# A replanned attention stage: other groups, other engines for two operations, zeros written in parts

## The chip, the cores and the metric

The kernel runs on one core of one Trainium2 chip. The metric is device time in microseconds (us) of one execution. TensorE (PE; PEld is its weight load) multiplies matrices, VectorE (DVE) and ScalarE (ACT) do elementwise work, GpSimd (POOL) does elementwise work and indirect DMAs, and SyncE (SP) only issues DMAs. SP's instructions run in the order of its queue, as on every engine.

## The reference

Three parts run one after the other on 1536 tokens (2 batches of 768) of width 384 (8 heads of 48).

```python
for t in range(S):                       # attention: a complex decay per channel
    new_re = ar*S_re - ai*S_im; new_im = ar*S_im + ai*S_re
    S_re, S_im = new_re + outer(k[t], v[t]), new_im
    y[t] = q[t] @ S_re
# first expert layer: argmax over 8 experts, at most 384 tokens each
h = relu(disp[e] @ w1[e]); out[i] = gate_w[i] * (h @ w2[e])[pos[i]]
# second layer, dense, 2048 wide
g = relu(h) + alpha*min(h, 0); out = g @ w_out      # h = x @ w_in
```

## The kernel before

The sequential attention is turned into matrix products over 12 tiles of 128 tokens. For each tile the kernel takes the magnitude and angle of the decay, sums their logarithms and turns along the tile, turns q and k with them, and then multiplies. The steps of tile i, each a function in the listing below:

- `log_polar(i)`: logarithm of the magnitude, with four Ln and Exp on ACT in the short form and one with a bias, products on DVE (L409, L423, L430), and one square (L414), which was on ACT.
- `decay(i)`: a product with a triangle on TensorE (L444), two Exp (L446, L447), each then squared three times: `ar` on ACT (L388), `ai` on POOL (L390).
- `edge(i)`: small transposes and products for the state at the tile's end (L466, L470).
- `turns(i)`: Arctan (L487), products (L492, L495), rounding (`r`, on ACT at L505 for even tiles and on DVE at L509 for odd ones), and the rest of a turn (L514).
- `rotate(i)`: two Sin (L528, L543), then `kk` and `qq` (L550, L555) on DVE. With these a tile is ready to be attended.
- `attend(i)`: for each half of the heads transposes of kk and qq (L580), their evictions on ACT (L585), scores (L599), a mask on DVE (L605), outputs (L614, L618), the state (L631).
- `route(g)`: logits of some tiles (L698), choice of expert, and a scatter of their rows by POOL into `xs_d` in DRAM (L769). Rows of `xs_d` that no token takes have to be zero, so `clear` writes zeros first. It also writes zeros into parts of `ys_d`, which the second layer gathers from, and into `gs_d`.

Ln and Exp need one activation table, Arctan and Sin another. So the tiles go in groups (`GROUPS`), and `stage` puts a table load (L355) ahead of each batch: one with decay of group g+1 and log_polar of group g+2, and one with turns of group g+2 and rotate of group g+1. The attend of group g goes beside them. A table load waits for all operations of the batch before it.

The order of instructions on each engine is written out by a planner (`Plan.order`). Every operation has an engine, a cost in us, dependences, buffers, and a rank: the tile's number plus an offset by kind (`RANK`). The planner goes through time; among the operations of an engine that can start within `SLACK` of the earliest, it takes the one of lowest rank. SP is one of these engines, with DMAs as operations. A dependence that is given to the planner alone (as `use` of a name that the function does not read) orders the plan, and puts no semaphore into the program. The weights of the first expert (`whole`, `preload`) are loaded and split in this stage too, at ranks 20 and 30.

Behind the attention stage the framework's own scheduler orders the work: for each of 8 experts a layer of three products per value (a high and a low part in fp32r), then three chunks of 512 tokens through the dense layer. A small gather of gates (`gsl<-gs_d`, L1149) waits for four scatters of POOL (L1134).

Of the kernel before, what the change touches and what calls it, by code (L numbers as in the profile page):

```python
# [21 lines left out]
P = 128  # L22
HD = 48
NH = 8
DM = NH * HD
VW = DM - HD + P
NE = 8
CAP = 384
SLOTS = 256
# [7 lines left out]
NTL = 12  # L37
C_TRI, C_TRIP, C_ONE, C_LAST, C_STRI, C_COL = (i * P for i in range(6))
C_IOT = C_COL + 2
C_TWIN = C_IOT + GT * NE  # L40
GROUPS = [[0], [1], [2, 3], [4, 5], [6, 7], [8, 9], [10, 11]]
RAW = {'ar': 6, 'ai': 6, 'q': 6, 'k': 4}
TMP = {'t1': 4, 't2': 3, 't3': 4, 'f': 4, 'r': 4, 'cs': 4, 'qq': 3}
ROUTES = [[0, 1, 2], [3, 4, 5], [6, 7], [8, 9], [10, 11]]
CW = C_TWIN + 4 * HD
LATE = [10, 11]
PS = {'pc': 2, 'y': 1, 'u': 1, 'tr': 2, 'sc': 2}
SQUARE = 'AAAAAAAAAAAA'
EVICT = 'AAAA'
DOUBLE = (('AAA', 'GGG'),) * NTL  # L50
TURN = 'AV' * 6
ABS = 'V' * NTL
C_ACT, C_BIAS, C_TT, C_STT, C_PS, C_WIDE, C_SQ = 0.415, 0.51, 0.47, 0.5, 0.47, 0.87, 0.79
LAG = {'A': 0.14, 'V': 0.13, 'G': 0.1, 'T': 0.28, 'S': 2.2}
SLACK = 0.02
LOOK = 1
RANK = {'L': -4.0, 'T': -3.5, 'D': -2.0, 'R': -1.5, 'E': -0.5, 'A': 0.0, 'O': 0.5}
FIRST = (4, 5)
CHT = 4
WIDE = 4  # L60
# [8 lines left out]
class Plan:  # L69
# [32 lines left out]
    def order(self):  # L102
        ops = self.ops
        n = len(ops)
        rest = [0.0] * n
        nexts = [[] for _ in ops]
        for i, o in enumerate(ops):
            for d in o["deps"]:
                nexts[d].append(i)
        for i in reversed(range(n)):  # L110
            rest[i] = ops[i]["cost"] + max([ops[i]["lag"] + rest[j] for j in nexts[i]], default=0.0)
        start, done = [None] * n, [None] * n
        free = {}
        slots = {t: [0.0] * b for t, b in self.bufs.items()}
        left = {v: len(u) for v, u in self.users.items()}
        last = {}
        waiting = [len(o["deps"]) for o in ops]
        ready = [i for i in range(n) if not waiting[i]]
        queue = {}
        for tag in self.bufs:  # L120
            queue[tag] = [i for i, o in enumerate(ops) for t, _ in o["new"] if t == tag]
        out = []
        while ready:
            best = []
            for i in ready:
                o = ops[i]
                t = max([free.get(o["engine"], 0.0), free.get("port", 0.0) if o["port"] else 0.0] + [done[d] for d in o["deps"]])
                ok = True
                need = {}
                for tag, _ in o["new"]:  # L130
                    need[tag] = need.get(tag, 0) + 1
                for tag, k in need.items():
                    if len(slots[tag]) < k or (tag not in self.loose and queue[tag][0] != i):
                        ok = False
                        break
                    t = max(t, sorted(slots[tag])[k - 1])
                if ok:
                    best.append((t, i))
            assert best, [(ops[i]["engine"], ops[i]["new"]) for i in ready]
            first = min(t for t, _ in best)  # L140
            engine = ops[min(best)[1]]["engine"]
            t, i = max(
                ((t, i) for t, i in best if ops[i]["engine"] == engine and t <= first + SLACK), key=lambda x: (-ops[x[1]]["rank"], rest[x[1]], -x[1])
            )
            o = ops[i]
            start[i] = t
            done[i] = t + o["cost"] + o["lag"]
            free[o["engine"]] = t + o["cost"]
            if o["port"]:
                free["port"] = t + o["cost"]  # L150
            for tag, v in o["new"]:
                slots[tag].remove(min(slots[tag]))
                queue[tag].remove(i)
            for v, u in self.users.items():
                if i in u:
                    left[v] -= 1
                    last[v] = max(last.get(v, 0.0), done[i])
                    if not left[v]:
                        slots[self.tagged[v]].append(last[v])
            ready.remove(i)  # L160
            for j in nexts[i]:
                waiting[j] -= 1
                if not waiting[j]:
                    ready.append(j)
            out.append((t, i))
        assert len(out) == n
        self.start, self.done = start, done
        return [i for _, i in sorted(out)]
# [22 lines left out]
def tile_kernel(  # L191
# [16 lines left out]
    nc = tc.nc  # L208
    V, A, G, T = nc.vector, nc.scalar.activation, nc.gpsimd, nc.tensor
    B, H, S, D = 2, NH, 768, HD  # L210
    NT = B * S
    ntile = S // P
    NTILE = NT // P
    groups = GROUPS
    NG = len(groups)
# [8 lines left out]
    ident = cpool.tile([P, P], F32, name="ident")  # L224
# [9 lines left out]
    alp = cpool.tile([P, 2 * FT], F32, name="alp")  # L234
# [5 lines left out]
    racc = cpool.tile([P, NE], F32, name="racc")  # L240
    xs_d = tc.dram_tile([NE * CAP, DM], F32, name="xs_d")
    ys_d = tc.dram_tile([NE * CAP + 1, DM], F32, name="ys_d")
# [62 lines left out]
    cst = acp.tile([P, CW], F32, name="cst")  # L305
# [4 lines left out]
    zero = acp.tile([P, DM], F32, name="zero")  # L310
# [24 lines left out]
    plan = Plan({**RAW, **TMP, "kk": TMP["qq"], "v": 6, "x": 6, "kT": 2, "qT": 2, "pT": 2, "xT": GT, "st": 3, **PS}, ("tr", "sc"))  # L335
    phase = {"load": None, "ops": []}

    def vector(cost, fn, **kw):
        return plan.op("V", cost, fn, **kw)
# [54 lines left out]
    def log_polar(i):  # L394
# [17 lines left out]
        def square():  # L412
            if SQUARE[i] == "A":
                A(out=t3(), in_=t2(), func=ACTF.Square)  # L414
# [257 lines left out]
    def route(g):  # L672
        tl_ = ROUTES[g]
        plan.rank = tl_[-1] + RANK["O"]
        n = len(tl_)
# [8 lines left out]
        for j, i in enumerate(tl_):  # L684
            p, x = f"px{i}", f"xT{i}"
# [78 lines left out]
        vector(1.2 + 0.25 * n, choose, use=[f"lg{g}", "racc", "ready"], put=["racc", f"oc{g}"])  # L764
        tensor(0.3, count, use=[f"oc{g}", "ready"], put=[f"pp{g}"], new=[("y" if tail else "u", f"pp{g}")])
        vector(2.0 if tl_[0] < CHT else 1.3, place, use=[f"pp{g}"], put=[f"si{g}"])
        for i in tl_:
            def scatter(i=i):
                ins = G.indirect_dma_start(  # L769
                    out=xs_d, out_offset=bass.IndirectOffsetOnAxis(ap=sidx[:, i:i + 1], axis=0),  # L770
                    in_=xt[i], in_offset=None, bounds_check=NE * CAP - 1, oob_is_err=False,
                )
                for p in scatters:
                    tc.declare_no_dep(ins.ins, p.ins, reason="the scattered rows are distinct")
                if tail:
                    for p in early:
                        tc.add_manual_dep(
                            ins.ins, p.ins.name, SYNC, reason="the first rows are read without the last tile's"
                        )
                scatters.append(ins)  # L780

            pool(1.2, scatter, use=[f"si{g}", f"x{i}", "zeroed"], put=[f"xs{i}"], lag=2.0, port=False)
# [69 lines left out]
    def sync(cost, put, **kw):  # L852
        plan.op("S", cost, lambda: nc.sync.dma_start(**kw), put=put, lag=2.2)

    def clear():
        nc.sync.dma_start(
            out=xs_d.rearrange("(p r) d -> p r d", p=P), in_=zero.unsqueeze(1).to_broadcast([P, NE * CAP // P, DM])
        )
        for e in range(NE):
            nc.sync.dma_start(out=ys_d[e * CAP + SLOTS:(e + 1) * CAP, :], in_=zero)  # L860
        for r in range((NE - 1) * CAP, (NE - 1) * CAP + SLOTS, P):
            nc.sync.dma_start(out=ys_d[r:r + P, :], in_=zero)
        nc.sync.dma_start(out=ys_d[NE * CAP:NE * CAP + 1, :], in_=zero[0:1])
        nc.sync.dma_start(out=gs_d.rearrange("(e c) o -> e (c o)", e=NE), in_=zero[0:NE, 0:CAP])

# [51 lines left out]
    sync(0.1, ["iotf"], out=iotf, in_=iota)  # L917
    sync(0.1, ["wg"], out=wg, in_=w_gate)
    sync(0.1, ["alp"], out=alp, in_=alpha)
    plan.op("V", 1.0, setup, use=["cst", "ident", "alp"], put=["racc", "ready"])  # L920
    routed = 0
    if LOOK:
        stage(6, (log_polar, 0), (decay, 0), (edge, 0), (log_polar, 1))
# [1 line left out]
    for g in range(NG):  # L925
        if g + 2 < NG:
            if g:
                load(g + 2, ("ar", "ai"))
            load(g + 2, ("q", "k"))
        if LOOK:  # L930
            if g + 1 < NG:
                stage(6, (decay, g + 1), (log_polar, g + 2), (edge, g + 1))
                stage(9, (turns, g + 2), (rotate, g + 1))
        else:
            stage(6, (log_polar, g), (decay, g), (edge, g))
            stage(9, (turns, g), (rotate, g))
        if g == 1:
            plan.op("S", 18.0, clear, use=["ar6", "k4"], put=["zeroed"], lag=2.2)
        for i in groups[g]:
            if i == LATE[0]:  # L940
                pool(2.5, gather_early, use=[f"xs{j}" for j in range(LATE[0])], put=["rows0a"], new=[("ar", "rows0a"), ("ar", "rows0b")])
            attend(i)
            if i == ROUTES[routed][-1]:
                route(routed)
                routed += 1
        if g + 2 < NG:
            load(g + 2, ("v",))
        if g in FIRST:
            whole(FIRST.index(g))
            if g == FIRST[-1]:  # L950
                preload()
# [343 lines left out]
```

## Time and profile before

| | us |
|---|---|
| median of 3 runs (lowest, highest) | 561.19 (559.08, 561.61) |
| profiled execution, its own time | 555.74 |
| its span, first to last instruction | 554.0 |
| TensorE busy in the span | 508.6 (92%) |
| VectorE, ScalarE, GpSimd busy | 336.1, 321.6, 71.7 |
| mean granted TensorE clock | 0.983 |

The attention stage ends at about 176.5 us of the span; from about 182 us the experts run. Busy time of TensorE says how long an instruction was in it, not how fast it ran: a slow instruction counts as long as it lasts. So counts of instructions per us are read beside it.

### The profile page before, as it was taken

Reading aid. Unit: us, or ns where it says so; the run is one execution under the profiler, and the core shown is the slowest. Engines: PE = TensorE matmul, PEld = TensorE weight load, DVE = VectorE, ACT = ScalarE, POOL = GpSimd, SP = SyncE. Lnnn points to the kernel's source line nnn. Section 1 sums busy time; section 2 is a strip of 40 time slices with the busy share of each in tenths; the row PEclk is TensorE's granted clock in tenths of the full one; section 3 lists DMA queues with packets and bytes.
Section 4 is the critical chain, followed back from the end, with each engine's and each line's share of the span. In section 5 each row is a group of like instructions: output and inputs, shape, how many; then the busy total and the mean of one; then the engine's idle time right before and its main releaser. Section 6 shows DMA issues by size and latency. Waiting matters only on the chain.

```text
span 554.0 us, 8596 instructions
## 1 busy us (share of the span) xinstructions
PE 508.6 (92%) x3270; PEld 466.2 (84%) x3270; DVE 336.1 (61%) x617; ACT 321.6 (58%) x601; POOL 71.7 (13%) x83
## 2 busy tenths in 40 slices
PE   1677999999998969999999998999999999999994
PEld 0466798888997958999999986988999989999993
DVE  2555889997663536676658969797933433333431
ACT  6589999995643346665656425464644534443432
POOL 2203126160512400000000020202000000000000
PEclk9978999999999989999999999999999999999998
DMA  8897534320001557788886466354101000100001
GB/s 270 291 397 253 147 101 157 116 87 0 30 12 47 114 173 246 230 249 264 268 304 188 143 200 205 105 160 135 54 0 58 1 0 1 43 15 1 1 0 63
DMA packets 37411, 71.04 MB, mean 128 GB/s; under 512 B 4105, under 2 KB 30098, under 8 KB 36594
## 3 DMA queue, kind: packets, MB, share of 16 engines
q1 hardware_dynamic: 35570, 65.30, 36.5%
q0 software_dynamic: 1792, 5.12, 2.8%
q8 instruction: 27, 0.44, 0.4%
q14 instruction: 22, 0.18, 0.1%
HBM read 55.84 MB, written 14.56 MB: 127 GB/s over the span
## 4 chain that ended last, share of the span: by engine, by line
PE 71%; DVE 10%; DMA 8%; ACT 6%; issue 2%; POOL 1%; SPq 0%; POOLq 0%; DVEq 0%; ACTq 0%
PE hp L1033 26%; PE y L1023 26%; PE y L614 3%; PE sc L599 3%; PE y L618 2%; PE u L631 2%; DMA gs_d<-gate,sidx 2%; PE pqT L580 1%; DMA sw<-in_moe_w_out 1%; DMA st<-in_moe_w 1%; DVE wl L294 1%; PE pt L492 1%; PE pt L1005 1%; DMA cst<-in_consts 1%; PE pkT L580 1%
## 5 line engine op out<-in xcount | busy, mean ns | idle before, releaser
L1023 PE MATMUL y<-wh,gh 128*128 128x384 f32 x320 | 109.6, 343 | 3.8 <-ACT gh L1041 3.8
L1033 PE MATMUL hp<-xl,wh 128*128 128x256 f32 (+1 forms) x336 | 111.0, 330 | 2.1 <-DVE xl L1008 1.0
L1033 PE MATMUL hp<-xh,wh 128*128 128x256 f32 (+1 forms) x336 | 111.5, 332 | 1.2 <-ACT xh L1007 1.0
L1033 PE MATMUL hp<-xh,wl 128*128 128x256 f32 (+1 forms) x336 | 110.8, 330 | 0.0
L1023 PE MATMUL y<-wl,gh 128*128 128x384 f32 x320 | 108.0, 337 | 0.0
L1023 PE MATMUL y<-wh,gl 128*128 128x384 f32 x320 | 89.3, 339 | 0.3 <-DVE gl L1042 0.2
L294 DVE TENSOR_TENSOR wl<-st,wh 128x768 fp32r<-128x768 f32 (+1 forms) x63 | 67.5, 1071 | 32.8 <-ACT wh L293 31.6
L293 ACT ACTIVATE wh<-st 128x768 fp32r<-128x768 f32 (+1 forms) x63 | 59.0, 936 | 28.8 <-DMA st<-in_moe_w 20.6
L1048 DVE SCALAR_TENSOR_TENSOR gn<-gn,nalp,gp 128x512 f32<-128x512 f32 x48 | 36.0, 749 | 62.5 <-ACT gp L1047 62.5
L1046 ACT ACTIVATE gn<-hp 128x512 f32<-128x512 f32 x48 | 28.7, 598 | 71.2 <-PE hp L1033 60.4
L1033 PEld LDWEIGHTS hp<-xl,wh 128*128 128x128 f32 x336 | 63.5, 189 | 7.6 <-DVE xl L1008 1.2
L1033 PEld LDWEIGHTS hp<-xh,wh 128*128 128x128 f32 x336 | 63.5, 189 | 7.1 <-ACT xh L1007 1.3
L1033 PEld LDWEIGHTS hp<-xh,wl 128*128 128x128 f32 x336 | 63.6, 189 | 5.0
L1023 PEld LDWEIGHTS y<-wh,gh 128*128 128x128 f32 x320 | 60.4, 189 | 5.6 <-ACT gh L1041 4.2
L1023 PEld LDWEIGHTS y<-wl,gh 128*128 128x128 f32 x320 | 60.6, 189 | 1.3
L1023 PEld LDWEIGHTS y<-wh,gl 128*128 128x128 f32 x320 | 57.0, 189 | 1.4 <-DVE gl L1042 0.9
L1050 DVE TENSOR_TENSOR gl<-gn,gh 128x512 fp32r<-128x512 f32 x48 | 33.2, 691 | 29.5 <-ACT gh L1049 29.5
L1041 ACT ACTIVATE gh<-hp 128x256 fp32r<-128x256 f32 x64 | 24.5, 383 | 44.0 <-PE hp L1033 39.6
L390 POOL TENSOR_TENSOR ai<-ai 128x384 f32<-128x384 f32 x36 | 34.9, 969 | 75.7 <-ACT ai L447 73.8
L1049 ACT ACTIVATE gh<-gn 128x512 fp32r<-128x512 f32 x48 | 30.2, 629 | 22.0 <-DVE gn L1048 21.9
L614 PE MATMUL y<-vt,pT 128*128 128x128 f32 x192 | 36.8, 284 | 2.3 <-DVE pT L605 2.2
L1042 DVE SCALAR_TENSOR_TENSOR gl<-hp,gh 128x256 fp32r<-128x256 f32 x64 | 26.7, 421 | 12.0 <-ACT gh L1041 11.8
(166 smaller groups left out, 810.8 us busy)
## 6 DMA issues: line engine op xcount, KB each, us to landing
st<-in_moe_w SPq DMA_DIRECT2D x24, 512.0 KB, 4.5
st<-in_moe_w SPq DMA_DIRECT2D x32, 384.0 KB, 3.9
sw<-in_moe_w_in SPq DMA_DIRECT2D x6, 1024.0 KB, 5.0
sw<-in_moe_w_out SPq DMA_DIRECT2D x8, 768.0 KB, 4.3
xs_d<-zero SPq DMA_DIRECT2D x1, 4608.0 KB, 15.6
ys_d<-o SPq DMA_DIRECT2D x16, 192.0 KB, 4.0
rows<-xs_d SPq DMA_DIRECT2D x14, 192.0 KB, 4.7
ar<-in_a_re SPq DMA_DIRECT2D x12, 192.0 KB, 3.5
```

Source lines behind the costliest of these rows:

```text
L293: follow(A(out=wh[:, js], in_=st, func=ACTF.Copy), behind, "A")
L294: ins = eng[j].tensor_tensor(out=wl[:, js], in0=st, in1=wh[:, js].bitcast(F32), op=ALU.subtract)
L390: (V if e == "V" else G).tensor_tensor(out=t, in0=t, in1=t, op=ALU.mult)
L614: T.matmul(out=y()[:, o:o + P], lhsT=tl[f"pT{i}{hh}"][:, h, :], rhs=tl[vk][:, o:o + P], start=True, stop=(c == 0))
L1023: T.matmul(out=ys[t], lhsT=a[:, sl], rhs=b[:, f, :], start=(ft == 0 and m == 0), stop=(ft == nf - 1 and m == 2))
L1033: ins = T.matmul(out=hp, lhsT=a[:, c, fs], rhs=b[:, c, :], start=(n == 0), stop=(n == 3 * KC - 1))
L1041: last["A"] = A(out=gh, in_=hp, func=ACTF.Relu)
L1042: last["V"] = V.scalar_tensor_tensor(out=gl, in0=hp, scalar=0.0, in1=gh.bitcast(F32), op0=ALU.max, op1=ALU.subtract)
L1046: A(out=gn, in_=hp, func=ACTF.Relu, scale=-1.0)
L1048: V.scalar_tensor_tensor(out=gn, in0=gn, scalar=nalp[:, ft:ft + 1], in1=gp, op0=ALU.mult, op1=ALU.add)
L1049: last["A"] = A(out=gh, in_=gn, func=ACTF.Copy)
L1050: last["V"] = V.tensor_tensor(out=gl, in0=gn, in1=gh.bitcast(F32), op=ALU.subtract)
```

## The change

Two elementwise operations go from ACT to DVE: all 12 squares of `log_polar` (`SQUARE`) and the 6 roundings of even tiles (`TURN`). The groups are 1, 2, 2, 2, 2, 2, 1 tiles instead of 1, 1, 2, 2, 2, 2, 2. The planner counts TensorE's operations 1.9 times and SP's 1.3 times as long before its time 22. The ranks of the kinds and the slack are others, and the six setup operations of DVE (L845 to L850) get the rank 3 and a cost of 2.2. `xs_d` is zeroed by four DMAs of 1152 KB with rank 3.5, planned behind `l4` (log_polar of tile 4), instead of one of 4608 KB. The zeros of `ys_d` and `gs_d` go behind the first routing in three operations at rank 40, in larger DMAs. The bytes written are the same.

```diff
-GROUPS = [[0], [1], [2, 3], [4, 5], [6, 7], [8, 9], [10, 11]]
+GROUPS = [[0], [1, 2], [3, 4], [5, 6], [7, 8], [9, 10], [11]]
-SQUARE = 'AAAAAAAAAAAA'
+SQUARE = 'V' * NTL
-TURN = 'AV' * 6
+TURN = 'V' * NTL
-SLACK = 0.02
+SLACK = 0.05
+CLEAR = {1: 'l4'}
+CLEAR_RANK = 3.5
+COLD, SLOW, EARLY, HEAVY = 22.0, 1.9, 22.0, 1.3
+SEED, NOISE = 0, 0.0
-RANK = {'L': -4.0, 'T': -3.5, 'D': -2.0, 'R': -1.5, 'E': -0.5, 'A': 0.0, 'O': 0.5}
+RANK = {'L': -4.9, 'T': -2.9, 'D': -3.5, 'R': -1.5, 'E': -2.5, 'A': -0.8, 'O': -0.5}
...
+            cost = o["cost"] * (SLOW if o["engine"] == "T" and t < COLD else HEAVY if o["engine"] == "S" and t < EARLY else 1)
-            done[i] = t + o["cost"] + o["lag"]
-            free[o["engine"]] = t + o["cost"]
+            done[i] = t + cost + o["lag"]
+            free[o["engine"]] = t + cost
...
-    def clear():
+    def clear(n):
+        r = NE * CAP // 4
         nc.sync.dma_start(
-            out=xs_d.rearrange("(p r) d -> p r d", p=P), in_=zero.unsqueeze(1).to_broadcast([P, NE * CAP // P, DM])
+            out=xs_d[n * r:(n + 1) * r, :].rearrange("(p r) d -> p r d", p=P),
+            in_=zero.unsqueeze(1).to_broadcast([P, r // P, DM]),
         )
-        for e in range(NE):
-            nc.sync.dma_start(out=ys_d[e * CAP + SLOTS:(e + 1) * CAP, :], in_=zero)
-        for r in range((NE - 1) * CAP, (NE - 1) * CAP + SLOTS, P):
-            nc.sync.dma_start(out=ys_d[r:r + P, :], in_=zero)
+
+    def clear_late(n):
+        if n < 2:
+            e = slice(n * NE // 2, (n + 1) * NE // 2)
+            nc.sync.dma_start(
+                out=ys_d[0:NE * CAP, :].rearrange("(e r) d -> r e d", r=CAP)[SLOTS:CAP, e, :],
+                in_=zero.unsqueeze(1).to_broadcast([P, NE // 2, DM]),
+            )
+            return
+        r = (NE - 1) * CAP
+        nc.sync.dma_start(
+            out=ys_d[r:r + SLOTS, :].rearrange("(t p) d -> p t d", p=P),
+            in_=zero.unsqueeze(1).to_broadcast([P, SLOTS // P, DM]),
+        )
...
+    plan.rank = 3.0
-    plan.op("V", 1.0, setup, use=["cst", "ident", "alp"], put=["racc", "ready"])
+    plan.op("V", 2.2, setup, use=["cst", "ident", "alp"], put=["racc", "ready"])
+    plan.rank = 0.0
...
-        if g == 1:
-            plan.op("S", 18.0, clear, use=["ar6", "k4"], put=["zeroed"], lag=2.2)
+        if g in CLEAR:
+            plan.rank = CLEAR_RANK
+            for n in range(4):
+                plan.op("S", 3.6, lambda n=n: clear(n), use=[CLEAR[g]], put=["zeroed"], lag=2.2)
+        if g == NG - 2:
+            plan.rank = 40.0
+            for n in range(3):
+                plan.op("S", 2.0, lambda n=n: clear_late(n), use=["si0"], lag=2.2)
```

## Rows read from the trace of the kernel before

**Rows 1.** The page's 40 slices of 13.85 us, busy share in tenths.
```profile
PE   1677999999998969999999998999999999999994
...
ACT  6589999995643346665656425464644534443432
```

**Rows 2.** Windows: from:to, length, busy us (instructions) of PE, PEld, DVE, ACT, POOL; clock.
```profile
22.00:38.00 16.00, 10.68 (x67) 9.16 (x66) 9.57 (x22) 12.09 (x25) 2.61 (x3) 0.79 1.03 374
38.00:58.00 20.00, 16.71 (x116) 14.20 (x115) 13.27 (x27) 18.46 (x38) 5.49 (x6) 0.91 0.73 246
58.00:126.00 68.00, 66.26 (x544) 59.08 (x543) 61.85 (x139) 66.58 (x135) 26.13 (x24) 1.00 0.40 123
126.00:176.50 50.50, 48.83 (x424) 45.30 (x423) 29.28 (x78) 25.19 (x48) 11.74 (x14) 1.00 0.07 25
```

**Rows 3.** Timeline of VectorE: start, duration; `kk` of tiles 0, 1 and 2.
```profile
20.67 0.96 DVE L555 TENSOR_TENSOR kk<-ai,cs 128x768 f32<-128x768 f32 x1 [0.70 <-ACT cs L543]
...
39.02 0.96 DVE L555 TENSOR_TENSOR kk<-ai,cs 128x768 f32<-128x768 f32 x1 [0.68 <-ACT cs L543]
...
57.43 0.94 DVE L555 TENSOR_TENSOR kk<-ai,cs 128x768 f32<-128x768 f32 x1
```

**Rows 4.** Timeline of ScalarE: four table loads, and two neighbours of one batch.
```profile
20.66 1.28 ACT L355 ACT_TABLE_LOAD   x1
...
34.85 1.28 ACT L355 ACT_TABLE_LOAD   x1
...
36.57 0.51 ACT L528 ACTIVATE cs<-f 128x384 f32<-128x384 f32 x1
36.99 0.51 ACT L487 ACTIVATE t<-t 128x384 f32<-128x384 f32 x1
...
39.01 1.28 ACT L355 ACT_TABLE_LOAD   x1
...
52.85 1.28 ACT L355 ACT_TABLE_LOAD   x1
```

**Rows 5.** Waits from 20 to 60 us: total, times, longest.
```profile
PE pz L466 <- ACT ar L388: 6.0, 2, 4.4
...
ACT w L414 <- DVE t L409: 2.9, 1, 2.9
```

**Rows 6.** Timeline of TensorE: neighbours of one kind at two places.
```profile
51.73 0.63 PE L614 MATMUL y<-vt,pT 128*128 128x128 f32 x2
52.15 0.63 PE L618 MATMUL y<-Z,qT 96*128 96x128 f32 x2
...
56.76 0.39 PE L618 MATMUL y<-Z,qT 96*128 96x128 f32 x2
56.98 0.39 PE L614 MATMUL y<-vt,pT 128*128 128x128 f32 x2
```

**Rows 7.** Timeline of SP's queue; the last row is the landing time of L856's DMA.
```profile
22.56 0.62 SPq L856 DMA_DIRECT2D xs_d<-zero  x1
23.22 15.24 SPq L860 DMA_DIRECT2D ys_d<-zero  x8
...
40.66 0.36 SPq L378 DMA_DIRECT2D k<-in_k  x1
...
DMA to landing us min/median/max: 15.6/15.6/15.6
```

**Rows 8.** Groups by line, 0 to 183 us: busy, mean ns; then L409's shortest, median, longest.
```profile
L414 ACT ACTIVATE w<-t 128x384 f32<-128x384 f32 x12 | 6.2, 521 | 3.5 <-DVE t L409 3.5
...
L505 ACT ACTIVATE r<-pt,bk 128x384 f32<-128x384 f32 x6 | 3.5, 580 | 2.4 <-PE pt L492 2.2 <-PE pt L495 0.2
L509 DVE TENSOR_SCALAR r<-pt 128x384 f32<-128x384 f32 x6 | 3.3, 553 | 2.4 <-PE pt L495 2.4
...
L409 DVE TENSOR_TENSOR t<-t,ai x12: 543/558/1184, 4.3 to 110.0; 128x384 f32<-128x384 f32 x12
```

**Rows 9.** The chain that ended last: start, duration, what.
```profile
188.19 8.69 DMA gs_d<-gate,sidx
```

More of the change, by code (lines that the diff above doesn't have):

```diff
@@ L112, in order @@
         start, done = [None] * n, [None] * n
+        order = np.random.default_rng(SEED).uniform(0, NOISE, n)
         free = {}
@@ L142, in order @@
             t, i = max(
-                ((t, i) for t, i in best if ops[i]["engine"] == engine and t <= first + SLACK), key=lambda x: (-ops[x[1]]["rank"], rest[x[1]], -x[1])
+                ((t, i) for t, i in best if ops[i]["engine"] == engine and t <= first + SLACK), key=lambda x: (-ops[x[1]]["rank"] - order[x[1]], rest[x[1]], -x[1])
             )
             o = ops[i]
+            cost = o["cost"] * (SLOW if o["engine"] == "T" and t < COLD else HEAVY if o["engine"] == "S" and t < EARLY else 1)
             start[i] = t
-            done[i] = t + o["cost"] + o["lag"]
-            free[o["engine"]] = t + o["cost"]
+            done[i] = t + cost + o["lag"]
+            free[o["engine"]] = t + cost
             if o["port"]:
-                free["port"] = t + o["cost"]
+                free["port"] = t + cost
             for tag, v in o["new"]:
@@ L766, in route @@
         vector(2.0 if tl_[0] < CHT else 1.3, place, use=[f"pp{g}"], put=[f"si{g}"])
+        assert "zeroed" in plan.writer
         for i in tl_:
```

## The prediction

> **What bounds the kernel now.** I read the page's slices first. TensorE is near full from the fifth slice to the end, with a dip in slices 13 to 15 (166 to 208 us) and a thin start; ScalarE is full from slice 4 to 9 and half empty after that [rows 1]. So only the thin start and the dip can give time back, and the edits all stand before the end of the dip's first slice.
>
> The windows size the start. From 58 to 126 us TensorE issues 544 instructions in 68 us, 8.0 per us, and from 126 to 176.5 us 424 in 50.5, 8.4 per us, at granted clock 1.00: here it is the bound. From 38 to 58 us it issues 116 where 8.0 per us would give 160, at clock 0.91, and from 22 to 38 us 67 where 128 would fit, at 0.79 [rows 2]. ScalarE is busy 18.46 of the 20 us from 38 to 58 and VectorE 13.27.
>
> The timeline says why TensorE is short there. A tile can be attended from its `kk` on, and `kk` of tiles 0, 1 and 2 come at 20.67, 39.02 and 57.43 us [rows 3]. They come with the second batch of each pair, so the pace is that of the table loads: 20.66, 34.85, 39.01, 52.85 [rows 4]. Between 39 and 57 us there is one tile, and TensorE has gaps. In them its clock falls: at 51.73 us two instructions take 0.42 us from start to start, at 56.76 us 0.22 [rows 6], that is 0.21 and 0.11 us each, the levels of 1.2 and 2.4 GHz. The waits of 20 to 60 us name ScalarE's squarings ahead of `pz` (6.0 us) and a ScalarE idle of 2.9 us behind L409 [rows 5]; none of the waits of TensorE, VectorE or ScalarE in that stretch is for a load.
>
> **Part by part: the groups.** With [1, 2] as the second group, tile 2 is rotated in tile 1's batch. What does this batch cost ScalarE more? In one batch neighbours start 0.42 us apart [rows 4], the pitch that I use. Tile 2's decay adds 2 Exp and 3 squarings (5 x 0.42 = 2.1 us), its two Sin 0.9. Its log_polar moves to the first pair of batches, where ScalarE has room while the first loads land. In return the squares of the two tiles in this batch's log_polar leave (0.84), and the idle of 2.9 us should shrink, since the setup operations that VectorE ran just before L409 have a later rank. So 2.1 + 0.9 - 0.84 = 2.2 us more, less 0 to 2.9: tile 2's `kk` at 39.02 + 0.95 (tile 1's qq) + (-0.7 to 2.2), about 39 to 42 us, and not 57.43. I take 41.
>
> From 41 us then TensorE has two tiles instead of one. The shortfall from 38 to 58 us is 160 - 116 = 44 instructions, 44 / 8.0 = 5.5 us. Three of the 20 us pass before tile 2 is there, so 17 / 20 of it can come back, 4.7 us, which I take; the ends are 0 (tile 2 as late as before) and 5.5. The next pair has to be there at about 41 + 19 = 60 us. ScalarE's work for it is the old batches' (39.01 to 57.43, 18.4 us) less two squares and one rounding (0.84 + 0.5), 17 us, plus the second tile's four evictions: 19 us, just in time. After that TensorE needs 24 us for two tiles (67 + 116 + 544 + 424 = 1151 instructions for 12 tiles [rows 2], 96 for one, 12 us at 8.0), ScalarE about 19, so ScalarE keeps ahead, and the gain of the start is carried to the end of the stage.
>
> **Squares and rounding.** ScalarE loses 12 x 0.521 + 6 x 0.580 = 9.7 us busy, VectorE gets 12 x 0.558 + 6 x 0.553 = 10.0 [rows 8]. About half falls into 58 to 126 us, where VectorE goes from 61.85 to some 66.9 of 68 and ScalarE from 66.58 to 61.7 [rows 2]. Neither is the bound while TensorE is at 66.26; the cover is that late elementwise work may slide into 126 to 176.5 us, where VectorE has 21 us free. Ends: -1 us (a hop between engines less in a chain) to +3 (VectorE passes TensorE). I take +0.3.
>
> POOL's squarings matter here: L409, also two SBUF inputs on VectorE, takes 0.558 us in the median and 1.184 at the longest, 0.626 more [rows 8]. At least half meet nothing, since the median lies beside the shortest (0.543): so 0 to 6 x 0.63 = 3.8 us on VectorE for the 12 squares, and I take 1, within the ends above.
>
> The Trainium skill speaks against the move at this place: SBUF — State Buffer, section "SBUF: two separate sides", says that a VectorE operation with two SBUF inputs and a GpSimd operation that reads SBUF hold one shared port pair in turn, each for its whole instruction, and that the other blocks. By that rule a square that meets a POOL squaring waits it out or holds it up; with POOL busy 26 of 68 us some 5 of 12 would, at 0.63 us each 3 us in place of 1, and the sum would be -3 and not -5. The longest L409 agrees with the rule; how often it happens only the median says.
>
> **Zeros.** SP issues the `xs_d` zeros at 22.56 and is held by the `ys_d` zeros until 38.5; loads go on at 40.66 [rows 7]. These loads were not waited for by the compute engines, so taking the zeros away there gives 0 by itself; at most, an early load lets the planner's earlier tile 2 have its q, k and v, which the sum above needs. The four new pieces last 15.6 / 4 = 3.9 us each and stand behind tile 4's log_polar, from about 35 to 60 us. Loads behind a piece come up to 3.9 us later. Queued behind them on SP are loads of tiles 5 to 8 and the weights; the first scatter needs all four, and on POOL the squarings of later tiles stand behind that scatter. It runs after tile 2's routing, at 60 us or later, so it is covered by about nothing to 10 us. I take 0; ends 0 and +7.8 (two pieces ahead of tile 5's or 6's load). The late `ys_d` zeros go into SP's gaps after the first routing; nothing needs them before the experts: 0.
>
> **Planner's factors, ranks and slack** move only the order; that the attend rank is lower puts evictions of tile 1 ahead of tile 6's log_polar, for TensorE, against the next batch. From -2 to +2, taken 0.
>
> **The first stretch.** From 22 to 38 us 61 instructions are missing (128 - 67), 7.6 us; what the change takes on there is ScalarE's idle of 2.9 us [rows 5], in which tile 0's evictions wait too. Half of it, at half the rate, is 0.7 us, which I take; ends 0 and 2.9.
>
> **Sum.** -4.7 + 0.3 - 0.7 = -5.1. From the stage's end to the end of the span, 554.0 - 176.5 = 377.5 us, I change nothing. The profiled execution goes from 555.74 to about 550.6. The runs' median is 561.19, 5.5 above that execution; on that footing the forecast is 556.1, rounded to 556.
>
> **The rivals.** (A) The forecast: tile 2 early. Own range 552 to 559.
>
> (B) The room at the start is not usable: the batch with two rotations ends late, or VectorE, at 66.9 of 68 plus 1 to 3 us for the port, becomes the bound. Then -5.1 becomes -2 to +1: 559 to 562, I say 560. For it: ScalarE has only 1.5 us free from 38 to 58 [rows 2], and its evictions stand between a ready tile and its scores. Against it: VectorE has 6.7 us free from 38 to 58.
>
> (C) Slower: two pieces of zeros stand ahead of the loads that log_polar of tiles 5 and 6 needs. The batch behind them, and all `kk` from tile 3 on, come 7.8 us late; TensorE runs dry near 60 us and the gain of 5 is lost: +2.6, 564. It decides from the point where that batch's first Ln starts after about 46 us. For it: the zeros move right into the stretch in which ScalarE is the pace. Against it: loads have the lower ranks there and go first.
>
> (D) More: also the stretch from 22 to 38 us becomes denser (half of its shortfall of 61 instructions is 3.8 us), or the framework's order of SP behind the stage changes, so that the chain's 8.69 us for `gs_d` [rows 9] no longer holds the weights. Then -9: 552 and below, 550.
>
> **How the numbers follow.** A 0.50, B 0.21, C 0.17, D 0.12. A measurement of this kernel can tell about 0.5% (2.8 us) from no change: faster is below 558.4, slower above 564.0. Faster is nearly all of A and all of D, 0.60; C and the worst orders give slower 0.17, though its centre sits on the bound, because a starved TensorE also gets the lower clock; the rest, 0.23, is the same. The range of 549 to 564 holds A and B, most of D, and half of C.
>
> **What would show it.** Right: tile 2's `kk` at 39 to 43 us, 145 or more TensorE instructions from 38 to 58 us, 0.11 us each in that stretch, the same 8.0 per us after it, and the stage's end 4 to 6 us earlier. Wrong: table loads later than 39 and 58 us; a VectorE above 67 of 68 us with TensorE waiting for the mask; a ScalarE that waits for loads between 40 and 60 us; or a difference behind 182 us, where I have none.

## The result and the profile after

The change takes 551.64 us in the median (550.78 to 551.86 in three runs; a fourth, 586.23 at a granted clock of 0.85, is left out) against 560.56 us before: ratio 0.9842, interval 0.9817 to 0.9867, 8.9 us less. Two repeats beside the kernel before gave 0.9822 (0.9779 to 0.9865) and 0.9856 (0.9831 to 0.9881). The forecast was 556, with a range of 549 to 564.

The profiled execution took 550.78 us (span 549.0), 5.0 less than before's 555.74. The gap between 5.0 and 8.9 is mostly in the execution of before that the profiler caught: it lies 4.8 us under its kernel's median, the change's only 0.9 under its own. Between its stores at 318.06 and 340.24 us, for example, before took 22.18 us and the change 24.11, the shortest and the longest of all profiles here (the twelve others took 22.40 to 23.97 for the same code). The start is steadier: the first store of an expert came at 208.39 us before, and at 200.35, 199.12 and 198.97 in three executions of the change, 8.0 to 9.4 earlier.

Slices of the changed kernel, 13.7 us each; the thin start of [rows 1] has shrunk to the first three slices, the dip remains.

```profile
PE   1889989999998779999999988999999999999994
```

Windows of the changed kernel, columns as in [rows 2]:

```profile
22.00:38.00 16.00, 13.59 (x89) 11.59 (x87) 12.56 (x32) 13.85 (x31) 5.90 (x6) 0.81 0.58 181
38.00:58.00 20.00, 20.00 (x165) 17.90 (x164) 17.30 (x32) 19.12 (x40) 5.64 (x6) 0.98 0.79 264
58.00:126.00 68.00, 66.02 (x542) 58.68 (x540) 61.17 (x142) 60.45 (x116) 25.23 (x24) 1.00 0.44 145
126.00:170.00 44.00, 42.70 (x369) 40.48 (x369) 27.74 (x82) 22.09 (x41) 10.25 (x11) 0.98 0.19 64
```

Read the first number in brackets, TensorE's instructions, against [rows 2]: 89 for 67, 165 for 116, 542 for 544. TensorE is 69 instructions ahead at 126 us, 8.2 us at its 8.4 per us. That is the change's gain, and all of it is earned between 22 and 58 us. The counts vary between executions: two more profiles of the change (e5_change_again, f1_change_third) have 89, 164, 547 and 89, 153, 548, so the lead at 126 us is 63 to 73 instructions. The last products of the stage, before and after, say the same in time:

```profile
174.50 0.39 PE L618 MATMUL y<-Z,qT 96*128 96x128 f32 x2
```

```profile
165.10 0.39 PE L624 MATMUL y<-Z,qT 96*128 96x128 f32 x2
```

The stage ends 9.4 us earlier (8.6 and 9.8 in the two other profiles), where the forecast had 4 to 6.

Timeline of VectorE after, for [rows 3]: `kk` of tiles 1 to 4.

```profile
37.48 0.95 DVE L561 TENSOR_TENSOR kk<-ai,cs 128x768 f32<-128x768 f32 x1
...
40.64 0.95 DVE L561 TENSOR_TENSOR kk<-ai,cs 128x768 f32<-128x768 f32 x1
...
57.74 0.96 DVE L561 TENSOR_TENSOR kk<-ai,cs 128x768 f32<-128x768 f32 x1 [0.63 <-ACT cs L549]
...
60.43 0.95 DVE L561 TENSOR_TENSOR kk<-ai,cs 128x768 f32<-128x768 f32 x1
```

Timeline of ScalarE after, for [rows 4]: the three table loads behind the one at 20.07 us.

```profile
32.28 1.28 ACT L361 ACT_TABLE_LOAD   x1
...
38.61 1.28 ACT L361 ACT_TABLE_LOAD   x1
...
53.66 1.28 ACT L361 ACT_TABLE_LOAD   x1
```

Tile 2 is there at 40.64 us and not at 57.43 (40.86 and 42.20 in the two other profiles), and the next pair at 57.74 and 60.43. The batch from 32.28 us rotates two tiles and still begins 2.6 us earlier than the old one-tile batch (34.85).

Why 22 to 38 us is denser shows in TensorE's timelines, first before, then after.

```profile
23.11 1.12 PE L580 MATMUL pkT<-ident,kk 128*96 128x128 f32 x8
...
29.99 0.46 PE L466 MATMUL pz<-ident,ar 32*96 32x32 f32 x4 [4.39 <-ACT ar L388]
...
33.99 3.35 PE L599 MATMUL sc<-qT,kT 96*128 96x128 f32 x16
37.18 1.06 PE L614 MATMUL y<-vt,pT 128*128 128x128 f32 x8
```

```profile
26.53 1.06 PE L605 MATMUL sc<-qT,kT 96*128 96x128 f32 x8
27.42 0.84 PE L637 MATMUL u<-vt,kk 128*96 128x96 f32 x8
...
31.36 0.37 PE L472 MATMUL pz<-ident,ar 32*96 32x32 f32 x4 [1.30 <-ACT ar L394]
...
32.65 2.05 PE L605 MATMUL sc<-qT,kT 96*128 96x128 f32 x8
...
46.02 0.39 PE L620 MATMUL y<-vt,pT 128*128 128x128 f32 x2
46.25 0.39 PE L624 MATMUL y<-Z,qT 96*128 96x128 f32 x2
```

Before, eight transposes at 23.11 us took 0.12 us each from start to start (to 24.07, the 2.4 GHz level), then came an idle of 4.39 us for ScalarE's squarings, and the 16 scores at 33.99 went at 0.20 each (3.19 to the next row), the 1.2 GHz level. After, scores at 26.53 go at 0.11 each; the wait for the squarings is down to 1.30 us; behind it, scores are slow again (2.05 for eight), and the slow rate lasts until about 38 us, in f1_change_third until about 41. From there on instructions stay at 0.11, as at 46.02.

### The profile page after: what moved, and what is told of

The parts are those of the page before. It is cut to its first block, busy times and chain, and to the rows that moved or that the text cites. A ratio compares the mean times of both kernels' runs of the same rounds, so it can differ in the third digit from the quotient of the medians.

```text
span 549.0 us, 8594 instructions
## 1 busy us (share of the span) xinstructions
PE 509.4 (93%) x3270; PEld 468.8 (85%) x3270; DVE 344.3 (63%) x635; ACT 314.6 (57%) x583; POOL 72.7 (13%) x83
## 4 chain that ended last, share of the span: by engine, by line
PE 78%; DVE 9%; DMA 7%; ACT 3%; issue 2%; POOL 1%; SPq 0%; POOLq 0%; ACTq 0%; DVEq 0%
PE hp L1060 29%; PE y L1050 28%; PE y L620 3%; PE sc L605 3%; PE y L624 2%; DMA st<-in_moe_w 2%; PE u L637 2%; DMA gs_d<-gate,sidx 2%; PE pt L498 2%; PE pqT L586 1%; PE pt L1032 1%; PE pkT L586 1%; DMA rows<-ys_d,eidx 1%; PE pt L501 1%; PE lg L704 1%
## 5 line engine op out<-in xcount | busy, mean ns | idle before, releaser
L396 POOL TENSOR_TENSOR ai<-ai 128x384 f32<-128x384 f32 x36 | 36.6, 1018 | 75.2 <-ACT ai L453 73.3
```

Source lines behind the costliest of these rows:

```text
L396: (V if e == "V" else G).tensor_tensor(out=t, in0=t, in1=t, op=ALU.mult)
```

## The experiments

All ratios are against runs of the kernel before on the same chip, medians 557.92, 558.36 and 557.88 us in the three sets; the forecast's steps are taken apart first. "Division" is which engine does the squares and the roundings. "Numbers" are the planner's: RANK, SLACK, the early factors (COLD, SLOW, EARLY, HEAVY), and the setup's cost and rank.

| kernel | groups | division | numbers | zeros | us | ratio (95%) |
|---|---|---|---|---|---|---|
| e4_before_new_groups | new | old | old | old | 563.96 | 1.0116 (1.0038, 1.0195) |
| e6_before_new_division | old | new | old | old | 557.18 | 0.9980 (0.9957, 1.0003) |
| e1_old_groups | old | new | new | new | 562.27 | 1.0086 (1.0052, 1.0120) |
| e2_old_division | new | old | new | new | 556.69 | 0.9985 (0.9944, 1.0027) |
| e7_old_planner_numbers | new | new | old | new | 559.87 | 1.0022 (0.9990, 1.0053) |
| f3_new_ranks_alone | new | new | RANK new | new | 554.24 | 0.9928 (0.9903, 0.9953) |
| e3_old_zeros | new | new | new | old | 552.33 | 0.9901 (0.9860, 0.9943) |
| f2_old_zeros_again | new | new | new | old | 550.38 | 0.9891 (0.9855, 0.9928) |
| e5_change_again | new | new | new | new | 548.44 | 0.9822 (0.9779, 0.9865) |
| f1_change_third | new | new | new | new | 549.49 | 0.9856 (0.9831, 0.9881) |

**The change without its groups** (e1_old_groups).

```diff
-GROUPS = [[0], [1, 2], [3, 4], [5, 6], [7, 8], [9, 10], [11]]
+GROUPS = [[0], [1], [2, 3], [4, 5], [6, 7], [8, 9], [10, 11]]
```

> The kernel after the change with the old groups (1, 1, 2, 2, 2, 2, 2 tiles) and all else kept. My theory (the second tile of the second group fills TensorE from 38 to 58 us): most of the gain goes. kk of tile 2 comes at 55 us or later and not at 40.6; TensorE issues 115 to 135 instructions from 38 to 58 us and not 165; the time is 555.5 to 559 against 551.6 of the change. Rival 1 (the operations taken off ScalarE are the gain) and rival 2 (the zeros out of SP's way, and the new ranks, are the gain): at most 1.5 us of it goes, 550.5 to 553.

562.27 us: slower than the kernel before, and more is lost than I had expected. Its windows:

```profile
22.00:38.00 16.00, 12.86 (x96) 10.36 (x95) 12.49 (x29) 14.19 (x28) 2.97 (x3) 1.00 0.34 104
38.00:58.00 20.00, 17.56 (x113) 15.22 (x113) 14.33 (x29) 17.11 (x35) 5.59 (x6) 0.83 0.52 174
58.00:126.00 68.00, 64.14 (x502) 55.87 (x501) 57.48 (x136) 56.81 (x112) 23.19 (x24) 0.97 0.54 184
```

The new division and numbers fill 22 to 38 us by themselves, 96 instructions at clock 1.00. But tile 2's `kk` comes at 51.01 us; 38 to 58 us has 113 instructions at clock 0.83, as thin as before. And 58 to 126 us, full in both other kernels, loses some 40; there tile 8's `kk` comes at 132.17 us, 27 us behind tile 7's. So the groups do carry the forecast's term for 38 to 58 us, and numbers that suit one grouping can starve TensorE later in another.

**The change without its division** (e2_old_division).

```diff
-SQUARE = 'V' * NTL
+SQUARE = 'AAAAAAAAAAAA'
-TURN = 'V' * NTL
+TURN = 'AV' * 6
```

> The kernel after the change with the squares and the even tiles' rounding back on ScalarE, all else kept. My theory: the batch that ends with tile 2's kk gets 0.84 us of ScalarE back and the next pair some 1.3, so kk of tile 2 comes 1 to 3 us later; the time is 552 to 554.5. Rival 1 (ScalarE's relief is the gain): ScalarE is the pace from 20 to 60 us and gets 9.7 us back, so that 5 us or more of the gain goes, 556.5 or more. Rival 3 (VectorE with the squares collides with GpSimd and costs): the time falls, under 550.5.

556.69 us: nearly all of the gain is gone, as much as rival 1 said, where I had costed this edit at 0.3 us. Windows, and TensorE's longest wait in the first of them:

```profile
22.00:38.00 16.00, 13.15 (x72) 10.80 (x71) 10.10 (x24) 14.43 (x31) 5.83 (x6) 0.77 0.47 148
38.00:58.00 20.00, 19.99 (x152) 17.70 (x151) 14.73 (x28) 16.35 (x35) 5.36 (x6) 0.93 0.69 236
58.00:126.00 68.00, 64.55 (x526) 57.29 (x525) 60.09 (x134) 61.42 (x121) 21.63 (x21) 1.00 0.53 176
```

```profile
30.38 0.37 PE L472 MATMUL pz<-ident,ar 32*96 32x32 f32 x4 [2.26 <-ACT ai L453]
```

With the squares on ScalarE the table loads of the first pair's rotation and of the next come at 34.93 and 59.79 us in place of 32.28 and 53.66. Tile 2 is early (45.21 us) but 4.6 later than in the change, and each stretch lacks instructions: 17, 13 and 16, together 46, 5.8 us at 8.0 per us. In the batch that ends at 34.93 us ScalarE is busy 13.51 of 14.66 us, in the change's 11.71 of 12.21: of the 2.4 us that it is longer, 1.8 are ScalarE's own work. In the rotation behind it ScalarE then waits 3.3 us for TensorE's `y`. So the squares lengthen ScalarE's batches, and a wait in the order that results adds to it.

**The change with the old zeros** (e3_old_zeros; once more as f2_old_zeros_again, beside a third run of the change).

```diff
-        if g in CLEAR:
-            plan.rank = CLEAR_RANK
-            for n in range(4):
-                plan.op("S", 3.6, lambda n=n: clear(n), use=[CLEAR[g]], put=["zeroed"], lag=2.2)
...
+        if g == 1:
+            plan.op("S", 18.0, clear, use=["ar6", "k4"], put=["zeroed"], lag=2.2)
```

> The kernel after the change with the zeros as before: one DMA of 4608 KB and all zeros of ys_d and gs_d behind it, at the early place in SP's order, all else kept. My theory: compute did not wait for loads in the kernel before, so the zeros cost 0 to 2 us: 551.5 to 553.5. But there are now five tiles' loads ahead of 60 us and not four; if k or q of tile 2 (or ar, ai of tiles 5 and 6) come behind the zeros, TensorE runs short from 38 to 58 us and the trace shows waits of ScalarE or VectorE for loads there; then rival 2 (the zeros are the gain) is right, with 555 or more.

> The kernel after the change with the zeros as before (one DMA of 4608 KB at the early place, the others behind it), on one chip with the change itself. The first time it was at 0.990 of the kernel before, on a chip where the change had no run. If the zeros carry a part of the gain (rival 2): 2.5 to 5 us slower than the change here, with TensorE even up to 58 us and fewer instructions from 58 to 126 us. If they carry none: within 1.5 us.

552.33 and 550.38 us. The second is 0.9 us over f1_change_third on one chip by the medians and 2.0 by the ratios, with overlapping intervals. From 22 to 58 us the two have 89 and 166, 89 and 158 instructions, as the change's profiles; from 58 to 126 us both have 527, where five profiles of the change's stage (its own three, and the two variants of the last experiment) have 542 to 553. In e3_old_zeros:

```profile
58.00:126.00 68.00, 64.36 (x527) 57.02 (x525) 62.05 (x140) 58.86 (x113) 27.37 (x24) 1.00 0.33 110
```

That is the sign that I had named for rival 2, and the stage ends at 166.82 and 167.76 us, 0.9 to 3.1 later than in those five. So the new zeros seem to carry 1 to 2 us of the gain, less than rival 2's 2.5 and not clear of noise in the time. No wait of a compute engine from 20 to 60 us is for a load, with the zeros at either place, so how they act is open. A piece is slower than my 3.9 us: the one whose landing the profile of the change shows took 6.6.

**The kernel before with the new groups alone** (e4_before_new_groups: the GROUPS line of the change in the kernel before).

> The kernel before the change with only the new groups (1, 2, 2, 2, 2, 2, 1). My theory: it has half or more of the gain, 553.5 to 557 against 560.6 of the kernel before, with kk of tile 2 at 41 to 44 us and 145 or more TensorE instructions from 38 to 58 us; what is left is the stretch from 22 to 38 us, where the old ranks still put evictions of tile 0 late. Rivals 1 and 2: no gain, 559 to 563, since ScalarE is as full as before and SP is held by the zeros from 22 to 40 us.

563.96 us, 6.0 slower, a miss on the wrong side, though tile 2 came early. Windows, then the timelines of ScalarE and VectorE:

```profile
38.00:58.00 20.00, 18.99 (x151) 16.48 (x150) 15.91 (x28) 19.55 (x41) 5.66 (x6) 1.00 0.89 297
58.00:126.00 68.00, 66.06 (x524) 57.00 (x524) 59.02 (x135) 61.32 (x121) 18.70 (x19) 0.97 0.35 115
126.00:170.00 44.00, 41.31 (x339) 38.43 (x338) 25.69 (x73) 23.93 (x45) 13.87 (x16) 0.92 0.08 28
```

```profile
50.55 0.52 ACT L408 ACTIVATE t<-l 128x384 f32<-128x384 f32 x1
...
54.72 1.05 ACT L889 ACTIVATE wh<-st 128x1024 fp32r<-128x1024 f32 x1
...
63.55 1.28 ACT L355 ACT_TABLE_LOAD   x1
```

```profile
56.30 0.55 DVE L409 TENSOR_TENSOR t<-t,ai 128x384 f32<-128x384 f32 x1
```

Tile 2 is there at 42.83 us and 38 to 58 us holds 151 instructions. But two things stand ahead of the next rotation. The log_polar of tile 6, which its table load waits for, is late on VectorE: L409, whose input is written at 51.07 us, runs at 56.30. And four conversions of expert weights (L889, 54.72 to 62.31) stand among its steps on ScalarE. The table load comes at 63.55 and tile 3's `kk` at 68.57, 11 us after the change's. The last group, tile 11 alone, gets its `kk` at 156.80 (144.72 in the change): from 126 to 170 us there are 339 instructions, 44 fewer than before's 383 in the same stretch, 5.2 us. An early tile was given back by two late ones. By 170 us this kernel is only 13 instructions behind before and its stage ends 1.4 us later; where the rest of the 6.0 us goes was not followed.

**The kernel before with the new division alone** (e6_before_new_division).

> The kernel before with only the squares and roundings on VectorE; old groups, ranks and zeros. My theory now (a pair of conditions: the second group brings the tile, and ScalarE's relief brings the batch behind it in time): alone the relief has no tile to feed TensorE with before the pair of tiles 2 and 3, so at most 2.5 us better than the kernel before, 555 to 559 where that is at 558, and 110 to 135 TensorE instructions from 38 to 58 us. Rival 1 (ScalarE's relief is the gain by itself): 553 or less, with the old groups.

557.18 us: 0.2%, as expected and not clear of noise, with 104 instructions from 38 to 58 us, a little under my bounds. Tile 2's `kk` comes at 54.75, so there is no tile to fill that stretch; ScalarE's room comes later, from 58 to 126 us (57.82 us busy for 66.58).

```profile
38.00:58.00 20.00, 16.93 (x104) 14.14 (x104) 14.27 (x26) 18.58 (x36) 6.14 (x6) 0.83 0.76 248
```

**The change with the old planner's numbers** (e7_old_planner_numbers).

```diff
-SLACK = 0.05
+SLACK = 0.02
-COLD, SLOW, EARLY, HEAVY = 22.0, 1.9, 22.0, 1.3
+COLD, SLOW, EARLY, HEAVY = 22.0, 1.0, 22.0, 1.0
-RANK = {'L': -4.9, 'T': -2.9, 'D': -3.5, 'R': -1.5, 'E': -2.5, 'A': -0.8, 'O': -0.5}
+RANK = {'L': -4.0, 'T': -3.5, 'D': -2.0, 'R': -1.5, 'E': -0.5, 'A': 0.0, 'O': 0.5}
...
-    plan.rank = 3.0
-    plan.op("V", 2.2, setup, use=["cst", "ident", "alp"], put=["racc", "ready"])
+    plan.op("V", 1.0, setup, use=["cst", "ident", "alp"], put=["racc", "ready"])
```

> The kernel after the change with the old ranks, the old slack, no factor for early costs and the old cost and rank of the setup; the new groups, division and zeros are kept. My theory (pair of conditions, the planner's numbers move only the order): 550.5 to 555, that is at most 4 us of the gain goes, most of it from 22 to 38 us. Rival 4 (the ranks are a third condition: with the old ones log_polar of the second tile of a group stands too late in VectorE's order, as in the kernel before with new groups, where its L409 ran at 56.3 us and the table load at 63.6): 557 or more, and the fifth and sixth table loads after the start come at 58 us or later.

559.87 us: all of the gain is gone, a miss for my theory and right for rival 4; its table loads come at 59.06 and 63.15 us. Windows, then TensorE's timeline:

```profile
22.00:38.00 16.00, 13.79 (x92) 10.70 (x90) 12.77 (x29) 11.86 (x27) 5.88 (x6) 1.00 0.28 82
38.00:58.00 20.00, 17.48 (x116) 14.48 (x116) 14.38 (x26) 17.49 (x36) 5.68 (x6) 0.83 0.73 254
```

```profile
36.62 0.55 PE L696 MATMUL px<-ident,x 128*128 128x128 f32 x3 [0.52 <-ACT x L656]
40.52 1.65 PE L498 MATMUL pt<-t,cst 128*128 128x384 f32 x2 [3.35 <-ACT t L493]
...
44.52 1.56 PE L586 MATMUL pkT<-ident,kk 128*96 128x128 f32 x8
45.91 0.84 PE L637 MATMUL u<-vt,kk 128*96 128x96 f32 x8
```

TensorE runs through tile 0 by 36.6 us (92 instructions, more than in the change), then has nothing until the rotation's batch, whose table load stands at 38.23 and not at 32.28. It idles 3.35 us, its clock falls (its instructions from 40.52 to 45.91 take 5.39 us, where the change's rates, 0.65 us for two of `pt` and 0.43 for four of `pkT`, give 2.8), and 48 or 49 instructions of 38 to 58 us are missing, just the change's gain there. Tile 2's `kk` at 43.95 us is early and no use, since tile 1 (41.41) is no earlier. Why the table load is late shows on VectorE, in the log_polar of tile 4, here and then in the change:

```profile
29.43 1.18 DVE L415 TENSOR_TENSOR t<-t,ai 128x384 f32<-128x384 f32 x1
...
34.61 1.02 DVE L422 TENSOR_TENSOR w<-t 128x384 f32<-128x384 f32 x1
```

```profile
23.40 1.02 DVE L415 TENSOR_TENSOR t<-t,ai 128x384 f32<-128x384 f32 x2
24.34 1.02 DVE L422 TENSOR_TENSOR w<-t 128x384 f32<-128x384 f32 x2
```

With the old numbers masks, a rotation's products and the setup go ahead of it; with the new ones it runs beside tile 3's, the square 10 us earlier. That is rival 4's mechanism, one batch sooner than it said.

**Which of the numbers** (f3_new_ranks_alone: the same kernel with the new RANK).

> The kernel of the run with the old planner numbers, and of those numbers only the ranks new: new groups, division, zeros and ranks; old slack, no early factors, old cost and rank of the setup. If the ranks are the third condition: within 3 us of the change, and tile 2's kk at about 38 to 41 us and not at 44. If the factors for the early stretch and the setup's place are what orders it: 556 or more, as with the old numbers (559.9), and the second table load of the second pair (32.3 us in the change, 38.2 with the old numbers) stays at 36 us or later.

554.24 us, between the two: 0.9% (5 us) better than e7_old_planner_numbers by the ratios, and 4.7 us short of f1_change_third beside it. The batch begins at 34.62 us, tiles 1 and 2 are there at 39.74 and 43.33, and 38 to 58 us has 154 instructions, as f1_change_third (153). What is missing is mostly in the first stretch, 71 for the change's 89 (and 14 of 548 from 58 to 126 us), with one wait of TensorE for ScalarE's squarings:

```profile
33.70 0.37 PE L472 MATMUL pz<-ident,ar 32*96 32x32 f32 x4 [3.02 <-ACT ar L394]
```

So the ranks bring tile 4's log_polar (24.93 and 25.86 us) and with it the batch forward, and the early factors, the slack and the setup's place, not told apart here, take the idle of 22 to 38 us away.

**Behind the stage: what holds the first experts' weights.** The change leaves the wait of [rows 9] in place. The chain of waits after, then the chains of two variants of the change at that place: the load of `gsl` on GpSimd's queue and not SP's (e8_gates_by_gpsimd), and in addition the four scatters held behind expert 2's stores (f4_gates_later).

```diff
-        ins = nc.sync.dma_start(
+        ins = G.dma_start(
             out=gsl, in_=gs_d[(NE - 1) * CAP:(NE - 1) * CAP + SLOTS, :].rearrange("(t p) o -> p (t o)", p=P)
```

```diff
                 tc.declare_no_dep(ins.ins, p.ins, reason="the scattered gates are distinct")
+            tc.add_manual_dep(ins.ins, stores[-1].ins.name, SYNC, reason="the loads of the first experts go first")
...
-            if e == 0:
+            if e == 3:
                 scatter_gates()
```

> The kernel after the change, but the small load of the gates from gs_d is issued by GpSimd behind its four scatters, and not by SP, where it waits for them in front of four loads of weights. If that wait holds the weights of expert 1 (SP issues the four loads at 189.6 us in the change, and the first of them is wanted at about 187): the loads go out at about 180 us, TensorE no longer waits 2.9 and 1.2 us for gh near 190 and 194 us, and the time falls by 3 to 6 us against the change, to 545 to 548. If the loads are bound by their own buffers or by the DMA engines: 0 to 1 us.

> The kernel after the change, with GpSimd's four scatters of the gates held back until the results of expert 2 are stored, and the load of the gates issued by GpSimd. When only the load went to GpSimd, SP issued the weights' loads at once, but the one issued at 178.9 us took 10.2 us to land beside the scatters. If the scatters' small writes are what holds it: the loads land in 4 to 5 us, ScalarE's wait for st between 180 and 190 us (8.2 us) falls under 3, and the time is 4 to 7 us under the change, 541 to 545 where that is at 548. If something else holds these loads (the gathers of rows, the scatter of the last tile's rows): 0 to 2 us under the change. A third way: the scatters now hold loads of expert 4 or 5 and cost there what they save here.

```profile
178.94 10.09 DMA gs_d<-gate,sidx
...
189.55 3.36 DMA st<-in_moe_w
```

```profile
178.94 10.19 DMA st<-in_moe_w
```

```profile
178.93 4.30 DMA st<-in_moe_w
```

e8_gates_by_gpsimd takes 547.02 us (0.9804, 0.9752 to 0.9855), 1.4 below the change in its set with overlapping intervals, so between its two forecasts; f4_gates_later 546.56 us (0.9802, 0.9775 to 0.9829), 2.9 below the change in its set, the best of all but short of its expectation. The rows say why the first was small: freed from SP's queue, the weights' load starts early but takes 10.19 us to land while the four scatters of single gates are under way; with the scatters gone it takes 4.30 (one profile each). The first store of an expert moves from 198.97 us (f1_change_third) to 193.45, 5.5 earlier. Part of that is paid again where the scatters now run: from 236 to 262 us ScalarE waits 8.3 us for weights, where the change has no such wait from 244 to 270.

## Why the prediction was right, and where it was not

**Right: the mechanism and the cover.** The thin start is what came back; 145 or more instructions were asked for from 38 to 58 us and 153 to 165 came, at 0.11 us each once the slow rate had ended; 58 to 126 us kept its 8.0 per us; from 20 to 60 us no compute engine waited for a load. Tile 2 was forecast at 41 us and came at 40.64, partly by two errors against each other: the rotation began 2.6 us earlier than before, and tile 2 came 3.2 us behind tile 1 where the forecast had 2. Rival C did not happen: the loads behind the zeros were in time, and the zeros in their new place gave 1 to 2 us, if anything, and cost none. Nor did B: VectorE did not become the bound.

**Mis-sized: two terms of the sum.** The time came out at -8.9 us, where rival D had -9, and outside A's own range of 552 to 559. The term of -4.7 for 38 to 58 us measured 49 instructions, 6.1 us (37, 4.6 us, in f1_change_third): I let the gain begin at tile 2's `kk`, but tile 1 too came earlier (37.48 for 39.02), and TensorE ran over the rate of 8.0 that I took as full (165 in 20 us, 8.25). The term of -0.7 for the first stretch measured 22 instructions in all three profiles, 2.75 us, at its bound of 2.9. I had counted only ScalarE's idle behind L409; the wait for the squarings went from 6.0 [rows 5] to 1.3 us as well:

```profile
PE pz L472 <- ACT ar L394: 1.3, 1, 1.3
```

and without it TensorE kept the fast level until 31 us. That is the first half of rival D, which I held for 0.12; its other half, the chain behind the stage, did not shrink (10.09 us for 8.69).

The terms by their measure are -6.1 - 2.75 + 0.25 (two instructions fewer from 58 to 126 us), -8.6, against -8.0 at the first store of an expert in the two profiles and -8.4 to -9.9 in the three sets of medians. The 1.4 us between the stage's end (-9.4) and that store (-8.0) are what the chain took longer. My step from the profiled execution to the median (add 5.5) was wrong, since the change's profile lies only 0.9 under its median. That the forecast on its own footing, 550.6, meets the profiled 550.78 is luck: the stage gave 9.4 and not 5.1, and that pair of profiles loses 4.4 behind it.

**Wrong: costing the edits one by one.** "Squares and rounding" stood in the sum at +0.3, the planner's numbers at 0 within -2 and +2. Undone alone, the first costs 1.3 to 1.6%, 7 to 9 us (ratio 0.9985 against 0.9822 and 0.9856; its set has no run of the change), the second 11.4 us (559.87 against 548.44 in one set). Put in alone, the division gives 1.2 us, within the noise, and the groups lose 6.0. The groups need the division, which gives ScalarE the time for a batch of two tiles, and the ranks, with which VectorE runs the log_polar that the next table load waits for in time. The step that failed is the one that read the groups' term as theirs alone; its sum came out near because all the conditions were in the change together.

**Squares and the port.** VectorE was to reach 66.9 of 68 us from 58 to 126 us, and has 61.17. Five of the 12 squares do fall there, but other work of VectorE has moved ahead with the tiles: from 22 to 58 us its busy time went from 22.8 to 29.9. The two lines with two SBUF inputs that may meet POOL's squarings, by line (ns shortest/median/longest):

```profile
L422 DVE TENSOR_TENSOR w<-t x12: 544/550/1067, 4.9 to 117.7; 128x384 f32<-128x384 f32 x12
```

```profile
L415 DVE TENSOR_TENSOR t<-t,ai x12: 546/551/944, 4.3 to 117.0; 128x384 f32<-128x384 f32 x12
```

With means of 593 and 587 ns the stretching costs 12 x 0.049 + 12 x 0.041 = 1.1 us for all 24, of which I had taken 1 for the moved 12. The Trainium skill (SBUF — State Buffer, section "SBUF: two separate sides") lets a VectorE operation with two SBUF inputs and a GpSimd operation that reads SBUF hold one port pair in turn; the longest instructions agree with that. My 5 in 12 from POOL's busy share took the two engines' operations as placed by chance, and they are not: the planner gives these lines and POOL's squarings a common resource (`port` in the listing) and plans no two of them for the same time. By the timelines only three of the 24 meet a squaring (46.85, 117.04 and 117.66 us), and two of those are the long ones, 0.94 and 1.07 us.

**Open.** Which of slack, factors and setup's place closes the first stretch was not tried, nor which of the ranks. The differences of e1_old_groups and e2_old_division from the change rest on two sets of runs, by their ratios. How much the zeros carry, and how, is not settled.

## What to carry to other kernels

An earlier input is worth something only if the next one is in time too: before you credit a reordering, follow the producer's batches to the one after, and to the last. Edits to a static order are conditions of each other, so price the stretch that they fill together, from the bound engine's instructions that are missing there, and not edit by edit. And ask of a short wait what it does to TensorE's rate behind it: here an idle of 3.35 us cost 2.6 more in slow instructions behind it.

## What was not expected of the hardware

Gaps of 3.35 us (e7_old_planner_numbers) and 4.39 us (before) were each followed by TensorE instructions at the 1.2 GHz level, in e7_old_planner_numbers until 45.9 us, though its granted clock from 22 to 38 us was 1.00. In the change instructions were at that level behind one of 1.30 us among small transposes (32 columns), at 31.36; in f1_change_third behind one of 1.34 at 32.82. What in those stretches brings the level down was not tested.

Four indirect scatters of 128 single gates each went with a weights' load on another queue that landed after 10.19 us; without them, the load at that place in the chain took 4.30.
